# Making the last group's first dense product beside its keys and queries instead of inside the output phase

## The chip, the cores and the metric

The kernel runs on one core of one Trainium2 chip; the rounds of runs were on different chips, and in each the kernel before ran beside the others. The metric is the device time of one execution in microseconds (us). A ratio is the mean time of one kernel's fast runs over the mean of the other's fast runs of the same rounds, with a 95% interval; it is therefore not quite the ratio of the medians quoted beside it.

Engine names are those of the profile: PE (matrix products), PEld (loading a product's stationary operand), DVE (vector), ACT (activation functions), POOL, and SP, which starts most of the DMA transfers. A "product" below is one PE instruction, for example 128x128 times 128x512.

## The reference

The computation is `x + A(xn) + B(xn)` with `xn = layernorm(x)`, 2048 tokens of width 512 in bfloat16.

```python
xn = _layernorm(x)
# A: linear attention, 32 heads of width 16
q, k, v = split(xn @ wqkv)
phi_q = concat(softmax(q @ w_phi), softmax(-(q @ w_phi)))
phi_k = concat(softmax(k @ w_phi), softmax(-(k @ w_phi)))
kv, z = phi_k^T v, sum(phi_k)            # over all tokens
A = (phi_q kv) / (phi_q z + 1e-6) @ wo
# B: two dense products
h = xn @ w1 + b1                          # 512 -> 1792
B = (h * tanh(softplus(h))) @ w2          # Mish, 1792 -> 512
```

`kv` and `z` are sums over all tokens, so no attention output can be made before the keys of the last tokens are done. B has no such dependency.

## The kernel before: what matters here

The tokens are worked in 4 groups of 512. For each group the kernel makes keys and values (`stage_kv_pair`, twice), queries (`stage_q`), the layer norm of the next group (`stage_ln`), the group's share of the sums (`stage_kvacc`), and the first dense product with Mish (`stage_h`). Then comes the output phase: attention output (`stage_o`) and, accumulated in one PSUM tile, the second dense product and the product with `wo` (`stage_out`). Before the change, the last group's `stage_h` stands in the output phase.

```python
# PSUM, 128 x 512 fp32 is one bank
ps_kq = pool(bufs=2)   # tiles of 2 banks: pk, pq, ph, pnd   ("big")
ps_v  = pool(bufs=2)   # tiles of 1 bank:  pv, po, pf
ps_m  = pool(bufs=2)   # tiles of 1 bank:  pS, pkv, transposes

def stage_kv_pair(xnT, pr):          # 256 tokens
    pk = big("pk"); ...              # 8 products of 512 columns
    ek[:, 0] = Exp(pk); ek[:, 1] = Exp(-pk)                    # ACT
    for tt in range(2):
        pv = bank_v("pv"); ...       # 4 products
        ss = reduce_sum(ek); rk = reciprocal(ss)               # DVE
        v12[:, :, :, 0:DH] = pv * rk                           # DVE, frees pv
        ...
def stage_q(g, xnT):
    for jp in range(2):
        pq = big("pq"); ...          # 8 products
        eq[:, 0] = Exp(pq); eq[:, 1] = Exp(-pq)                # ACT
        ...                          # 4 times: pS = B16b x eq (PE), eqT = pS * eq (DVE)
def stage_h(xnT):
    act = apool.tile([P, FT, 512], BF16, name="act")
    for fp in range(FT // 2):        # 7 pairs
        ph = big("ph"); ...          # 8 products
        ...                          # 2 x act = Mish(ph + b1)   (ACT)
    return act
def stage_o(g):
    for t in range(TPG):
        pnd = big("pnd"); ...        # 8 products of 136 columns: eqT x kvm
        rd = reciprocal(...); o_t = pnd * rd                   # DVE
    ...                              # 16 transposes ptro (PE), 2 copies oT (ACT)
def stage_out(g, act, oT):
    for t in range(TPG):
        po = bank_v("po")
        ...                          # 14 products act x w2, then 4 products oT x wo
        y = po + x; store(y)

for g in range(NG):
    parts = [stage_kv_pair(xnT, pr) for pr in range(2)]
    ...
    stage_q(g, xnT)
    if g + 1 < NG:
        ...; xnTs[g + 1] = stage_ln(g + 1)
    stage_kvacc(g, parts)
    if g + 1 == NG:
        break
    acts[g] = stage_h(xnT)
... # kvm = masked sums (DVE)
for g in range(NG):
    oT = stage_o(g)
    stage_out(g, acts[g], oT)
    if g == 0:
        acts[NG - 1] = stage_h(xnTs[NG - 1])
```

The framework's scheduler decides at compile time in which order the stages' instructions stand on each engine. So the program's text is not the order on PE; below, orders are told as the compiled program has them. A product that waits holds up all products behind it: the Trainium skill, "PSUM — Partial Sum Buffer", section "Engine vs sequencer instructions", says that matrix products start and complete in program order, and the traces here agree: in the longest wait looked at in group 3 (2.91 us) no product starts on PE.

The softmax here doesn't subtract the row's maximum and nothing guards it: scores larger than these inputs give would overflow.

Of the kernel before, what the change touches and what calls it, by code (L numbers as in the profile page):

```python
# [8 lines left out]
BF16 = mybir.dt.bfloat16  # L9
# [8 lines left out]
def kernel(  # L18
# [13 lines left out]
    P = 128  # L32
    S, D, NH, DH, F = 2048, 512, 32, 16, 1792
    NG = 4
# [3 lines left out]
    FT = F // P  # L38
# [20 lines left out]
    xnpool = ctx.enter_context(tc.tile_pool(name="xn", bufs=4))  # L59
    xnTpool = ctx.enter_context(tc.tile_pool(name="xnT", bufs=2))  # L60
    spool = ctx.enter_context(tc.tile_pool(name="small", bufs=4))
    ekpool = ctx.enter_context(tc.tile_pool(name="ek", bufs=4))
    eqpool = ctx.enter_context(tc.tile_pool(name="eq", bufs=2))
    vpool = ctx.enter_context(tc.tile_pool(name="v12", bufs=6))
    apool = ctx.enter_context(tc.tile_pool(name="act", bufs=3))

    prep_w = tc.alloc_tile_pool(name="prep_w", bufs=1)
# [71 lines left out]
    def chain(ins):  # L139

        prev = last_of.get("act")
        last_of["act"] = ins
        if prev is not None:
            tc.add_manual_dep(
                ins.ins,
                prev.ins.name,
                mybir.DependencyInfo(
                    mybir.DependencyClass.NoSync, mybir.DependencyReason.DATA
                ),
                reason="table order",  # L150
            )

    def big(name):
        return ps_kq.tile([P, 2, 512], FP32, name=name, tag="kq")
# [8 lines left out]
    def stage_ln(g):  # L163
        xg = xgs[g]
        mv = spool.tile([P, TPG, nc.vector.BN_AGGR_DIM], FP32, name="mv")
        rstd = spool.tile([P, TPG], FP32, name="rstd")
        for t in range(TPG):
            st = spool.tile([P, nc.vector.BN_STATS_DIM], FP32, name="st")
            nc.vector.bn_stats(st[:], xg[:, t, :])  # L169
            nc.vector.bn_aggr(mv[:, t, :], st[:])  # L170
        chain(nc.scalar.activation(rstd[:], mv[:, :, 1], ACT.Sqrt, bias=eps_t[:]))  # L171
        nc.vector.reciprocal(rstd[:], rstd[:])
        xns = []
        for t in range(TPG):
            xn = xnpool.tile([P, D], BF16, name="xn")
            nc.vector.tensor_scalar(  # L176
                out=xn[:],
                in0=xg[:, t, :],
                scalar1=mv[:, t, 0:1],
                scalar2=rstd[:, t : t + 1],  # L180
                op0=ALU.subtract,
                op1=ALU.mult,
            )
            xns.append(xn)
        xnT = xnTpool.tile([P, KT, 512], BF16, name="xnT")
        for kh in range(2):
            ptr = bank_m("ptr", [P, 2, 512], BF16)
            for t in range(TPG):
                for k in range(2):
                    kt = 2 * kh + k  # L190
                    nc.tensor.transpose(  # L191
                        ptr[:, k, t * P : (t + 1) * P],
                        xns[t][:, kt * P : (kt + 1) * P],
                        ident[:],
                    )
            nc.scalar.copy(xnT[:, 2 * kh : 2 * kh + 2, :], ptr[:])
        return xnT
# [12 lines left out]
    def fold(src, dst):  # L210
        wTs = []
        for jh in range(2):
            ptr = bank_m("ptrw", [P, 2, 512], BF16)
            for jj in range(2):
                j = 2 * jh + jj
                for kt in range(KT):
                    nc.tensor.transpose(
                        ptr[:, jj, kt * P : (kt + 1) * P],
                        src[:, kt, j * P : (j + 1) * P],
                        ident[:],  # L220
                    )
            wT = prep_w.tile([P, 2, 512], BF16, name="wT", bufs=2)
            nc.scalar.copy(wT[:], ptr[:])
            wTs.append(wT)
        for kt in range(KT):
            pf = bank_v("pf")
            for j in range(4):
                nc.tensor.matmul(
                    pf[:, j * P : (j + 1) * P],
                    lhsT=wTs[j // 2][:, j % 2, kt * P : (kt + 1) * P],  # L230
                    rhs=Wbd[:, j, :],
                    start=True,
                    stop=True,
                )
            nc.vector.tensor_copy(dst[:, kt, :], pf[:])
# [76 lines left out]
    def stage_q(g, xnT):  # L312
        gs = slice(g * 512, (g + 1) * 512)
        for jp in range(2):
            pq = big("pq")
            for jj in range(2):
                j = 2 * jp + jj
                for kt in range(KT):
                    nc.tensor.matmul(  # L319
                        pq[:, jj, :],  # L320
                        lhsT=wqp[:, kt, j * P : (j + 1) * P],
                        rhs=xnT[:, kt, :],
                        start=(kt == 0),
                        stop=(kt == KT - 1),
                    )
            eq = eqpool.tile([P, 2, 2, 512], BF16, name="eq")
            chain(nc.scalar.activation(eq[:, 0], pq[:], ACT.Exp))  # L327
            chain(nc.scalar.activation(eq[:, 1], pq[:], ACT.Exp, scale=-1.0))  # L328
            for jj in range(2):
                j = 2 * jp + jj  # L330
                for pl in range(2):
                    pS = bank_m("pS")
                    nc.tensor.matmul(  # L333
                        pS[:],
                        lhsT=B16b[:],
                        rhs=eq[:, 1 - pl, jj, :],
                        start=True,
                        stop=True,
                    )
                    nc.vector.tensor_tensor(  # L340
                        out=eqT[:, pl * 4 + j, gs],
                        in0=pS[:],
                        in1=eq[:, pl, jj, :],
                        op=ALU.mult,
                    )


    def stage_h(xnT):
        act = apool.tile([P, FT, 512], BF16, name="act")
        for fp in range(FT // 2):  # L350
            ph = big("ph")
            for ff in range(2):
                f = 2 * fp + ff
                for kt in range(KT):
                    nc.tensor.matmul(  # L355
                        ph[:, ff, :],
                        lhsT=w1_sb[:, kt, f * P : (f + 1) * P],
                        rhs=xnT[:, kt, :],
                        start=(kt == 0),
                        stop=(kt == KT - 1),  # L360
                    )
            for ff in range(2):
                f = 2 * fp + ff
                chain(
                    nc.scalar.activation(  # L365
                        act[:, f, :], ph[:, ff, :], ACT.Mish, bias=b1f[:, f : f + 1]
                    )
                )
        return act
# [68 lines left out]
    xnTs = [None] * NG  # L438
    acts = [None] * NG
# [5 lines left out]
    for g in range(NG):  # L445
        xnT = xnTs[g]
        parts = [stage_kv_pair(xnT, pr) for pr in range(2)]
        if g == 0:
            fold(wq_raw, wqp)
            prep_w.release()  # L450
            oTpool = ctx.enter_context(tc.tile_pool(name="oT", bufs=2))
            rpool = ctx.enter_context(tc.tile_pool(name="rden", bufs=4))
            opool = ctx.enter_context(tc.tile_pool(name="o_t", bufs=5))
            ypool = ctx.enter_context(tc.tile_pool(name="y", bufs=3))
        stage_q(g, xnT)
        if g + 1 < NG:
            if g + 1 > 1:
                xgs[g + 1] = xpool.tile([P, TPG, D], BF16, name="xg")
                nc.sync.dma_start(xgs[g + 1][:], x_g[g + 1])
            xnTs[g + 1] = stage_ln(g + 1)  # L460
        stage_kvacc(g, parts)
        if g + 1 == NG:
            break
        acts[g] = stage_h(xnT)

    kvv = kvacc[:].rearrange("p s (h v) -> p s h v", v=VW)
    nc.vector.tensor_scalar(
# [12 lines left out]
    for g in range(NG):  # L480
        oT = stage_o(g)
        stage_out(g, acts[g], oT)
        if g == 0:
            acts[NG - 1] = stage_h(xnTs[NG - 1])


# [28 lines left out]
```

## Time and profile before

| | before |
|---|---|
| median time, 3 runs | 231.58 us |
| span of the profiled run | 229.3 us |
| PE busy | 197.9 us, 86% |

These lines are of the profile's page: PE's busy time and instructions, PE's busy tenths in 40 slices of the span, the granted PE clock in tenths, and the engines' shares of the chain that ended last.

```profile
PE 197.9 (86%) x1185; PEld 99.1 (43%) x1185; DVE 120.2 (52%) x205; ACT 101.3 (44%) x124; POOL 8.5 (4%) x26
...
PE   0089168889999999999999599899999999999993
...
PEclk9999977999999999999999979999999999999999
...
PE 61%; ACT 18%; DVE 12%; issue 4%; DMA 3%; SPq 1%; ACTq 0%
```

Counting the slices from 0, PE is busy 90% or more in every slice from 9 on except 22, 25 and the last, and it carries 61% of the chain. There is one dent left, in slices 22 to 25 (126 to 149 us), with a clock of 7 tenths in one slice: the last group's keys and queries and the start of the output phase.

The timeline there (start, duration, engine, line, instruction, count; in brackets the engine's idle time before it and what ended it):

```profile
127.17 1.89 PE L258 MATMUL pv<-wv,xnT 128*128 128x512 bf16 x8
...
130.76 1.17 DVE L274 TENSOR_TENSOR v_1202<-pv,rk 128x1024 bf16<-128x1024 f32 x1
...
131.97 3.54 PE L418 MATMUL po<-w_sb,act 128*128 128x512 bf16 x9 [2.91 <-DVE v_1202 L274]
...
143.24 1.11 PE L380 MATMUL pnd<-kvm,eqT 128*128 128x136 bf16 x16 [0.23 <-DVE kvm L474]
...
145.05 0.65 PE L380 MATMUL pnd<-kvm,eqT 128*128 128x136 bf16 x8 [0.71 <-DVE o_t L391]
...
146.53 0.90 PE L403 MATMUL ptro<-ident,o_t 128*128 128x128 bf16 x8
...
147.27 1.03 PE L355 MATMUL ph<-xnT,w_sb 128*128 128x512 bf16 x4
```

Two gaps are to be seen. First: the second `pv` ends at about 129.1 us, and the next work on PE is the first output product `po`. It needs a PSUM bank of `ps_v`, and both are held by `pv` until DVE has made `v_1202`. PE stands for 2.91 us. After it, 9 products take 3.54 us. Second: from 143.2 to 147 us `pnd` waits for `kvm` (0.23 us) and for `o_t` (0.71 us), and the transposes `ptro` come one by one with DVE's `o_t`; only 4 dense products (`ph`) stand between the last of them, and 5 more behind.

The windows table (stretch; length; busy time and count of each engine; granted PE clock; DMA share and GB/s), with stretches cut at these places:

```profile
core 0: us, PE busy (x) PEld busy (x) DVE busy (x) ACT busy (x) POOL busy (x), PEclk, DMA share, GB/s
...
129.06:131.97 2.91, 0.00 (x1) 0.00 (x0) 2.91 (x5) 0.00 (x0) 0.86 (x2) 0.92 0.00 0
131.97:135.14 3.17, 3.17 (x9) 1.09 (x9) 2.27 (x3) 0.00 (x0) 0.00 (x0) 0.54 0.00 0
...
149.51:170.15 20.64, 20.64 (x96) 9.21 (x96) 2.67 (x4) 9.74 (x14) 0.00 (x0) 1.00 0.15 51
170.15:188.13 17.98, 17.96 (x117) 9.04 (x116) 6.08 (x11) 3.19 (x4) 0.00 (x0) 1.00 0.07 23
```

The rows are the wait (PE busy 0.00 us of 2.91), the 9 products after it (granted clock 0.54), the first output group from its first `wo` product to the end of the late dense product, and the second output group from its first to the third's first `pnd`. In the last two PE is busy all the time. At full rate one product of 512 columns starts every 0.216 us (40 take 8.63 us), at half rate every 0.43 us.

### The profile page before, as it was taken

What the parts mean: (1) busy time and instruction counts of PE and PEld (TensorE: products, weight loads), DVE (VectorE), ACT (ScalarE), POOL (GpSimd) and SP (SyncE); (2) the same over time, 40 slices, a digit from 0 to 9 for tenths busy, and PEclk for the clock granted to TensorE, in tenths of its full rate; (3) what the DMA queues carried; (4) which work ended last, traced back from release to release, by engine and by line L of the source; (5) the groups of instructions that cost most, each with busy time, mean ns of one, the idle gap of its engine ahead of it and who ended that gap; (6) DMA issues with size and microseconds to landing.
All of it is one profiled execution on the core that took longest, in us unless ns stands there. A gap on an engine that the chain in (4) does not pass through costs nothing.

```text
span 229.3 us, 2898 instructions
## 1 busy us (share of the span) xinstructions
PE 197.9 (86%) x1185; PEld 99.1 (43%) x1185; DVE 120.2 (52%) x205; ACT 101.3 (44%) x124; POOL 8.5 (4%) x26
## 2 busy tenths in 40 slices
PE   0089168889999999999999599899999999999993
PEld 0065024355444364443644236544455455446441
DVE  1538798667069951699516978622015226217121
ACT  0266500995889677896778400142663002000300
POOL 2000110000011000110001100000000000000000
PEclk9999977999999999999999979999999999999999
DMA  6999100011000030000200000010300103010001
GB/s 169 363 363 348 43 0 0 1 46 48 0 0 1 0 93 2 0 0 3 91 0 3 0 0 1 0 49 23 114 0 3 46 23 117 23 46 26 23 26 43
DMA packets 12120, 12.25 MB, mean 53 GB/s; under 512 B 1100, under 2 KB 12108, under 8 KB 12108
## 3 DMA queue, kind: packets, MB, share of 16 engines
q1 hardware_dynamic: 10496, 11.01, 14.6%
q10 hardware_dynamic: 1612, 1.07, 1.7%
q8 instruction: 9, 0.15, 0.3%
q14 instruction: 3, 0.02, 0.0%
HBM read 9.98 MB, written 2.10 MB: 53 GB/s over the span
## 4 chain that ended last, share of the span: by engine, by line
PE 61%; ACT 18%; DVE 12%; issue 4%; DMA 3%; SPq 1%; ACTq 0%
PE po L418 21%; PE ph L355 17%; PE po L426 6%; DVE ss L266 5%; PE pkv L294 3%; ACT act L365 3%; PE pq L319 3%; PE pnd L380 3%; DMA xg<-in_A_x_dram 3%; ACT L251 2%; ACT L171 2%; PE ptr L191 2%; ACT ek L252 2%; ACT ek L251 2%; ACT eq L327 2%
## 5 line engine op out<-in xcount | busy, mean ns | idle before, releaser
L418 PE MATMUL po<-w_sb,act 128*128 128x512 bf16 x224 | 56.0, 386 | 2.9 <-DVE v_1202 L274 2.9
L355 PE MATMUL ph<-xnT,w_sb 128*128 128x512 bf16 x224 | 54.7, 379 | 1.7 <-ACT act L365 1.7
L365 ACT ACTIVATE act<-ph,b1f 128x512 bf16<-128x512 f32 x56 | 35.2, 686 | 22.9 <-PE ph L355 15.7
L434 DVE TENSOR_TENSOR y<-po,xg 128x512 bf16<-128x512 f32 x16 | 11.0, 691 | 44.7 <-PE po L426 44.7
L418 PEld LDWEIGHTS <-act 128*128 128x128 bf16 x224 | 21.7, 99 | 27.3 <-issue 5.5
L355 PEld LDWEIGHTS <-w_sb 128*128 128x128 bf16 x224 | 21.6, 98 | 26.4 <-issue 2.7
L408 ACT COPY oT<-ptro 128x1024 bf16<-128x1024 bf16 x8 | 7.7, 1015 | 56.3 <-PE ptro L403 56.3
L266 DVE TENSOR_REDUCE ss<-ek 128x64 f32<-128x1024 bf16 x16 | 18.7, 1212 | 24.2 <-ACT ek L252 24.2
L340 DVE TENSOR_TENSOR eqT<-pS,eq 128x512 bf16<-128x512 f32 x32 | 20.5, 687 | 4.1 <-PE pS L333 4.1
L258 PE MATMUL pv<-wv,xnT 128*128 128x512 bf16 x64 | 16.9, 404 | 4.8 <-DVE v_260 L274 4.8
L319 PE MATMUL pq<-xnT,wqp 128*128 128x512 bf16 x64 | 16.6, 405 | 0.9 <-ACT ek L252 0.9
L426 PE MATMUL po<-wo_sb,oT 128*128 128x512 bf16 x64 | 16.9, 380 | 0.0
L191 PE MATMUL ptr<-ident,xn 128*128 128x128 bf16 x64 | 6.1, 242 | 11.3 <-DVE xn L176 11.3
L243 PE MATMUL pk<-wkp,xnT 128*128 128x512 bf16 x64 | 15.4, 379 | 0.0
L327 ACT ACTIVATE eq<-pq 128x1024 bf16<-128x1024 f32 x8 | 8.2, 1027 | 14.9 <-PE pq L319 14.3
L169 DVE BATCH_NORM_STATS2 st<-xg 128x6 f32<-128x512 bf16 x16 | 10.5, 674 | 5.9 <-DMA xg<-in_A_x_dram 5.9
L333 PE MATMUL pS<-eq,B16b 128*128 128x512 bf16 x32 | 11.5, 378 | 0.9 <-ACT eq L328 0.9
L258 PEld LDWEIGHTS <-xnT 128*128 128x128 bf16 x64 | 6.5, 102 | 13.2 <-issue 6.2
L389 DVE RECIPROCAL rd<-pnd 128x32 f32<-128x32 f32 x16 | 5.6, 349 | 11.5 <-PE pnd L380 11.5
L391 DVE TENSOR_TENSOR o_t<-pnd,rd 128x512 bf16<-128x512 f32 x16 | 11.1, 692 | 0.5
L319 PEld LDWEIGHTS <-wqp 128*128 128x128 bf16 x64 | 6.6, 104 | 9.2 <-issue 3.1
L380 PE MATMUL pnd<-kvm,eqT 128*128 128x136 bf16 x128 | 9.6, 223 | 1.1 <-DVE o_t L391 0.7
(96 smaller groups left out, 197.0 us busy)
## 6 DMA issues: line engine op xcount, KB each, us to landing
xg<-in_A_x_dram SPq DMA_DIRECT2D x7, 512.0 KB, 4.0
out_dram<-y SPq DMA_DIRECT2D x16, 128.0 KB, 1.7
w_sb<-in_B_w_dram SPq DMA_DIRECT2D x2, 896.0 KB, 7.8
w_sb<-in_B_w_dram SPq DMA_DIRECT2D x1, 1792.0 KB, 13.5
wk_raw<-in_A_wqkv_dram ACTq DMA_DIRECT2D x1, 512.0 KB, 4.6
xg<-in_A_x_dram SPq DMA_DIRECT2D x4, 128.0 KB, 4.8
wq_raw<-in_A_wqkv_dram ACTq DMA_DIRECT2D x1, 512.0 KB, 6.9
wv<-in_A_wqkv_dram SPq DMA_DIRECT2D x1, 512.0 KB, 7.2
```

What stands on the lines that cost most here:

```text
L243: nc.tensor.matmul(pk[:, tt, :], lhsT=xnT[:, kt, tok0 : tok0 + P], rhs=wkp[:, kt, :], start=(kt == 0), stop=(kt == KT - 1),)
L258: nc.tensor.matmul(pv[:], lhsT=xnT[:, kt, tok0 : tok0 + P], rhs=wv[:, kt, :], start=(kt == 0), stop=(kt == KT - 1),)
L266: nc.vector.reduce_sum(ss[:], ek[:, :, tt, :].rearrange("p s (h e) -> p s h e", e=DH), axis=AX.X,)
L319: nc.tensor.matmul(pq[:, jj, :], lhsT=wqp[:, kt, j * P : (j + 1) * P], rhs=xnT[:, kt, :], start=(kt == 0), stop=(kt == KT - 1),)
L327: chain(nc.scalar.activation(eq[:, 0], pq[:], ACT.Exp))
L333: nc.tensor.matmul(pS[:], lhsT=B16b[:], rhs=eq[:, 1 - pl, jj, :], start=True, stop=True,)
L340: nc.vector.tensor_tensor(out=eqT[:, pl * 4 + j, gs], in0=pS[:], in1=eq[:, pl, jj, :], op=ALU.mult,)
L355: nc.tensor.matmul(ph[:, ff, :], lhsT=w1_sb[:, kt, f * P : (f + 1) * P], rhs=xnT[:, kt, :], start=(kt == 0), stop=(kt == KT - 1),)
L365: nc.scalar.activation(act[:, f, :], ph[:, ff, :], ACT.Mish, bias=b1f[:, f : f + 1])
L380: nc.tensor.matmul(pnd[:, j // 2, (j % 2) * 136 : (j % 2) * 136 + 136], lhsT=eqT[:, pl * 4 + j, tok0 : tok0 + P], rhs=kvm[:, pl * 4 + j, : ...
L418: nc.tensor.matmul(po[:], lhsT=act[:, f, ts], rhs=w2_sb[:, f, :], start=(f == 0), stop=False,)
L426: nc.tensor.matmul(po[:], lhsT=oT[:, j, ts], rhs=wo_sb[:, j, :], start=False, stop=(j == 3),)
```

## The change

The intent: make the last group's first dense product next to its keys and queries, as in the other groups, so that PE has independent work there. All four activation tiles then live at once, so a fourth buffer is needed, and other pools are cut to make room in SBUF.

```diff
-    ekpool = ctx.enter_context(tc.tile_pool(name="ek", bufs=4))
+    ekpool = ctx.enter_context(tc.tile_pool(name="ek", bufs=3))
-    vpool = ctx.enter_context(tc.tile_pool(name="v12", bufs=6))
+    vpool = ctx.enter_context(tc.tile_pool(name="v12", bufs=5))
...
-    def stage_h(xnT):
-        act = apool.tile([P, FT, 512], BF16, name="act")
+    def stage_h(xnT, pool):
+        act = pool.tile([P, FT, 512], BF16, name="act")
...
             prep_w.release()
+            apool3 = ctx.enter_context(tc.tile_pool(name="act3", bufs=1))
...
-            opool = ctx.enter_context(tc.tile_pool(name="o_t", bufs=5))
-            ypool = ctx.enter_context(tc.tile_pool(name="y", bufs=3))
+            opool = ctx.enter_context(tc.tile_pool(name="o_t", bufs=4))
+            ypool = ctx.enter_context(tc.tile_pool(name="y", bufs=2))
...
         stage_kvacc(g, parts)
-        if g + 1 == NG:
-            break
-        acts[g] = stage_h(xnT)
+        acts[g] = stage_h(xnT, apool if g + 1 < NG else apool3)
...
         stage_out(g, acts[g], oT)
-        if g == 0:
-            acts[NG - 1] = stage_h(xnTs[NG - 1])
```

## The prediction

It was made before the changed kernel had run, from the profile of before and the compiled orders of both.

> **What bounds the kernel now.** The tensor engine. The page gives PE 86% of the span, and the chain of waits is 61% PE. From 149.5 us to the last product (windows 149.51 to 225.81) PE is busy without a gap; DVE and ACT are mostly idle there. In that stretch a 512-column product starts every 0.216 us (40 of the dense product take 8.63 us in the chain). So only idle or slow PE time can be saved; the change removes no PE work (both orders hold 1185 products).
>
> **Where PE time is lost before.** Group 3 and the start of the output phase, 117.54 to 149.51, hold 93 products of 512 columns, 64 of 136 and 16 transposes: my estimate at the full rate is 93x0.216 + 64x0.060 + 16x0.056 = 24.8 us, against 31.97 us. Of the 7.2 us lost:
> - 2.9 us: PE stands from 129.1 to 131.97, because the first output product needs a PSUM bank that DVE frees at the end of v_1202 (table of waits, timeline);
> - about 1.8 us: after this gap the granted clock is 0.50 from 132 to 134.9 us (windows) and products start every 0.43 us. The Trainium skill, "TensorE: Matmul & The Clock Gate", section "What's actually happening", says an idle PE falls to half clock; the trace agrees, after about 2.5 us idle;
> - about 1.8 us: from 142.9 to 148.1 kvm and then pnd to o_t to transposes run with little other PE work queued;
> - 0.5 us: second pq waits for ACT's exponentials; the rest is small change.
>
> **What the change moves.** By the compiled order, group 3's 56 dense products now fill the place after the second pv, as in group 2: pv x4, ph x2, pv x4, ph x14, po x4, ph x5, then ph between the pS; 24 more stand between pkv and the first pnd. All four output groups then have the order that group 1's has now. The smaller pools (ek 3, v12 5, o_t 4, y 2) add waits that should already be met: each buffer's last reader is done microseconds earlier. The fourth activation buffer only permits the move. Table loads stay equal in number.
>
> **Sum.** Everything up to the second pv of group 3 stays (pS starts at 126.75). Then pS, pv, ph 26 products to 132.35; po x4 needs its bank, free at 131.93, so no stall and no clock drop; ph x5, then 17 products to 138.0; pkv about 2.3 us to 140.3; ph x24 5.2 us to 145.5 (kvacc and kvm, 1.75+0.2+1.3 us on DVE, hide under it). From the first pnd on, the order equals before's from 170.15 us, plus one more output group of 18.74 us (188.13 to 206.87). Span: 145.5 + (229.3-170.15) + 18.74 = 223.3 us against 229.3, 6.0 us less. ACT is no limit: group 2 with its square root keeps a 28.7 us period, and group 3 has none (1.6 us less).
>
> Predicted time 225.6 us, range 224.7 to 227.1. Chances: faster by over 2% 0.86, within 2% 0.13, slower by over 2% 0.01. The order barely leaves room for a loss; the doubt is whether 2% (226.95 us) is passed.
>
> **What would show it.** No 2.9 us PE wait on v_1202's counterpart, granted clock 1.00 around 132 us, first pnd at about 145.5 us with no wait on kvm, four output groups of 18.0 to 18.9 us each, PE busy total slightly lower, last product ending near 220 us.
>
> **What would make it wrong.** The po x4 standing on DVE after all (its margin is about 0.4 us), with another clock drop; ph waiting on mish in group 3 as it does 0.55 us in group 2; a wait from the smaller pools (a y buffer on its store, or a v12 in groups 1 to 3) that appears in earlier groups; stage_o(0) no longer hidden.

## The result, and the profile after

The changed kernel took 226.07 us (median of 4 runs, 225.44 to 226.62); the kernel before 231.63 us beside it. The ratio is 0.9749 (0.9713 to 0.9786): 2.5% faster. Repeated with more rounds on another occasion it was 226.83 us, ratio 0.9743 (0.971 to 0.9777).

The same lines of the page after:

```profile
PE 197.7 (88%) x1185; PEld 100.1 (45%) x1185; DVE 120.4 (54%) x205; ACT 101.2 (45%) x124; POOL 8.6 (4%) x26
...
PE   0089455889999999999999999999999999999993
...
PEclk9999967999999999999999999999999999999999
...
PE 70%; ACT 15%; DVE 8%; DMA 2%; issue 2%; SPq 1%; ACTq 0%
```

PE's busy time is the same, as no work was removed. The dent in the slices of the last group is gone and PE's share of the chain rose from 61% to 70%: from 126.1 us to the last product the chain now runs on PE, where before it ran on ACT and DVE until 131.97 us and again from 140.7 to 147.0 us, but for 0.65 us of `pnd`. The clock's dip in the middle is gone; one near the start (slices 5 and 6), which before has too, remains.

The timeline of the same place:

```profile
130.51 3.19 PE L355 MATMUL ph<-xnT,w_sb 128*128 128x512 bf16 x14
...
131.87 1.17 DVE L274 TENSOR_TENSOR v_1205<-pv,rk 128x1024 bf16<-128x1024 f32 x1
...
133.53 1.03 PE L418 MATMUL po<-w_sb,act 128*128 128x512 bf16 x4
...
141.31 5.34 PE L355 MATMUL ph<-xnT,w_sb 128*128 128x512 bf16 x24
...
146.49 0.64 PE L380 MATMUL pnd<-kvm,eqT 128*128 128x136 bf16 x8
...
146.96 1.03 PE L418 MATMUL po<-w_sb,act 128*128 128x512 bf16 x4
...
148.00 1.11 PE L380 MATMUL pnd<-kvm,eqT 128*128 128x136 bf16 x16
```

Where PE stood idle there are now sixteen dense products, 2 between the halves of the second `pv` and 14 right behind it. `v_1205`, the counterpart of `v_1202`, ends at 133.04 us (131.87 + 1.17), and the first `po` starts at 133.53 us without a wait. Behind the sums (`pkv`) come 24 dense products while DVE makes `kvm`, and between the `pnd` there are now `po` products.

The windows: from the end of the second `pv` to the third `pS`, from there to the first `pnd`, and the first output group:

```profile
130.50:135.47 4.97, 4.97 (x24) 2.25 (x23) 4.86 (x7) 3.33 (x5) 0.88 (x2) 1.00 0.00 0
135.47:146.49 11.02, 11.02 (x75) 5.93 (x74) 6.83 (x11) 5.06 (x8) 0.00 (x0) 1.00 0.00 1
146.49:164.47 17.98, 17.96 (x118) 9.06 (x116) 6.08 (x11) 3.19 (x4) 0.00 (x0) 1.00 0.07 23
```

PE is busy throughout and the clock is 1.00. The last row is the first output group, from its first `pnd` to the next group's first `pnd`: 17.98 us, exactly what the second output group took before.

The profiled spans differ by 5.0 us, but the profiled run of after happened to reach group 3 later: its first `pk` of group 3 comes at 118.67 us, before's at 117.54 us. In all profiled runs of kernels that do not change group 0 or the start, this point lies anywhere between 117.1 and 119.5 us, with either set of buffers. So I compare from the first `pk` of group 3 to the end of the span (the span minus that start): **111.76 us before, 105.63 us after, 105.67 us in the repeated run**. The difference, 6.1 us, is what the change did; the repeated run shows that this measure holds within 0.04 us, while whole times spread by some 1%. The spans are given to 0.1 us, so a difference of less than about 0.1 us in it says nothing.

### The profile page after: what moved, and what is told of

Same layout as the page of the kernel before. It is cut to its first block, busy times and chain, and to the rows that moved or that the text cites. A ratio compares the mean times of both kernels' runs of the same rounds, so it can differ in the third digit from the quotient of the medians.

```text
span 224.3 us, 2903 instructions
## 1 busy us (share of the span) xinstructions
PE 197.7 (88%) x1185; PEld 100.1 (45%) x1185; DVE 120.4 (54%) x205; ACT 101.2 (45%) x124; POOL 8.6 (4%) x26
## 3 DMA queue, kind: packets, MB, share of 16 engines
q1 hardware_dynamic: 10496, 11.01, 15.0%
## 4 chain that ended last, share of the span: by engine, by line
PE 70%; ACT 15%; DVE 8%; DMA 2%; issue 2%; SPq 1%; ACTq 0%
PE po L418 22%; PE ph L355 17%; PE po L426 6%; DVE ss L266 5%; PE pkv L294 4%; PE pnd L380 4%; PE pq L319 3%; PE pv L258 3%; PE pk L243 3%; ACT eq L328 2%; DMA xg<-in_A_x_dram 2%; ACT L171 2%; PE pS L333 2%; PE ptr L191 2%; ACT ek L252 2%
## 5 line engine op out<-in xcount | busy, mean ns | idle before, releaser
L355 PE MATMUL ph<-xnT,w_sb 128*128 128x512 bf16 x224 | 55.5, 379 | 1.7 <-ACT act L365 1.7
L418 PE MATMUL po<-w_sb,act 128*128 128x512 bf16 x224 | 54.4, 379 | 0.0
L418 PEld LDWEIGHTS <-act 128*128 128x128 bf16 x224 | 21.2, 98 | 22.2
L243 PE MATMUL pk<-wkp,xnT 128*128 128x512 bf16 x64 | 15.9, 387 | 0.0
L327 ACT ACTIVATE eq<-pq 128x1024 bf16<-128x1024 f32 x8 | 8.2, 1028 | 14.9 <-PE pq L319 14.3
L191 PEld LDWEIGHTS <-xn 128*128 128x128 bf16 x64 | 4.4, 106 | 12.6 <-DVE xn L176 11.9
L196 ACT COPY xnT<-ptr 128x1024 bf16<-128x1024 bf16 x8 | 7.7, 1015 | 5.0 <-PE ptr L191 5.0
```

What stands on the lines that cost most here:

```text
L191: nc.tensor.transpose(ptr[:, k, t * P : (t + 1) * P], xns[t][:, kt * P : (kt + 1) * P], ident[:],)
L243: nc.tensor.matmul(pk[:, tt, :], lhsT=xnT[:, kt, tok0 : tok0 + P], rhs=wkp[:, kt, :], start=(kt == 0), stop=(kt == KT - 1),)
L355: nc.tensor.matmul(ph[:, ff, :], lhsT=w1_sb[:, kt, f * P : (f + 1) * P], rhs=xnT[:, kt, :], start=(kt == 0), stop=(kt == KT - 1),)
L418: nc.tensor.matmul(po[:], lhsT=act[:, f, ts], rhs=w2_sb[:, f, :], start=(f == 0), stop=False,)
```

## The experiments

The theory before the experiments: two stretches are filled, the wait for `v12` with the half clock behind it (4.6 us by the prediction's sum), and the stretch of `kvm`, `pnd` and `o_t` (about 1.8 us). Rivals: the gain comes from getting the dense product out of the output phase; or from the changed buffers; or the first gap is all.

| run | what | median us | ratio to before (95%) | first pk of group 3 to end of span, us |
|---|---|---|---|---|
| before | | 231.58 | 1 | 229.3 - 117.54 = 111.76 |
| after_again | the change | 226.83 | 0.9743 (0.971-0.9777) | 225.1 - 119.43 = 105.67 |
| e1_pools | buffers alone | 231.26 | 0.9982 (0.9918-1.0047) | 230.2 - 118.58 = 111.62 |
| e2_early4 | 4 of 7 pairs moved | 226.99 | 0.9748 (0.9713-0.9784) | 224.7 - 118.81 = 105.89 |
| e3_afterkv | moved, but behind the sums | 231.53 | 0.9962 (0.9913-1.001) | 229.0 - 117.53 = 111.47 |
| e4_junk | before, idle time filled with useless products | 231.26 | 0.9926 (0.9887-0.9964) | 229.8 - 119.52 = 110.28 |
| e5_bare | the change, output products used up early | 227.56 | 0.9805 (0.9748-0.9862) | 224.3 - 117.08 = 107.22 |

The medians are of different rounds; the median of before beside them was 232.95 us for after_again, e2_early4, e3_afterkv and e4_junk, and 232.25 us for e1_pools and e5_bare. The last column rests on one profiled run of each.

### The change again (after_again)

> The changed kernel once more, with more rounds. My theory (two stretches of idle or slow TensorE around the last group's keys and queries are filled, 5.9 us in all): ratio to before 0.972 to 0.977, and the group 3 stretch repeats (no PE wait for v12, clock 1.00, first pnd about 27.8 us after the first pk of group 3). Second question: the profiled run of the changed kernel spent 1.1 us more before group 1 (half-rate products from 12 to 19 us) than that of before. If that is chance of the clock at the start, this profile shows some other start, between 60.1 and 61.2 us for the first pk of group 1; if it belongs to the changed pools, it is at 61.2 us again.

Measured: 0.9743, clock 1.00, first `pnd` 27.81 us (147.24 - 119.43) after the first `pk`. On the second question, the first `pk` of group 1 came at 61.95 us, later than either; in e3_afterkv, with the same buffers, it came at 60.05 us. So the 1.1 us at the start belong to the single execution and not to the change.

### Buffers alone (e1_pools)

```diff
 # against the changed kernel
-        acts[g] = stage_h(xnT, apool if g + 1 < NG else apool3)
+        if g + 1 == NG:
+            break
+        acts[g] = stage_h(xnT, apool)
...
         stage_out(g, acts[g], oT)
+        if g == 0:
+            acts[NG - 1] = stage_h(xnTs[NG - 1], apool3)
```

> Only the buffers of the change (ek 3, v12 5, o_t 4, y 2, a fourth activation buffer), while the last group's dense product stays in the output phase. My theory: the buffers alone do nothing; ratio to before 0.995 to 1.005, first pnd 25.7 us after the first pk of group 3, and 111.8 us from that pk to the end of the span. Rival, that the smaller pools gain or lose time: outside that.

Measured: 0.9982, first `pnd` 25.56 us after the first `pk` (144.14 - 118.58), 111.62 us to the end. The buffers alone do nothing that can be seen (0.14 us).

### Four of the seven pairs (e2_early4)

```diff
 # against the changed kernel; stage_h takes a range of pairs
-        acts[g] = stage_h(xnT, apool if g + 1 < NG else apool3)
+        if g + 1 < NG:
+            acts[g] = stage_h(xnT, apool)
+        else:
+            acts[g] = stage_h(xnT, apool3, range(4))
...
         stage_out(g, acts[g], oT)
+        if g == 0:
+            stage_h(xnTs[NG - 1], apool3, range(4, FT // 2), acts[NG - 1])
```

> Half of the move: 4 of the 7 pairs of the last group's first dense product go next to keys and queries, 3 pairs stay in the output phase, pools as after. The compiled order then has dense products after the second pv as in the changed kernel, but after pkv come 9 output products instead of 24 dense ones. My theory: the first gap (2.9 us idle, 1.8 us of half clock) is gone, and the second (kvm, pnd, o_t) is filled too, by the output products which are no longer used up in the first: ratio 0.974 to 0.978, within 0.7 us of the changed kernel. Rival, that the second gap needs the dense product itself, or that the output phase runs better only without any dense product in it: only the first gap's 4.6 us are won, ratio 0.980 or higher.

Measured: 0.9748, 105.89 us, 0.24 us from the changed kernel. PE's timeline in this run:

```profile
141.45 2.10 PE L419 MATMUL po<-w_sb,act 128*128 128x512 bf16 x9
143.58 1.12 PE L381 MATMUL pnd<-kvm,eqT 128*128 128x136 bf16 x16
144.53 1.03 PE L419 MATMUL po<-w_sb,act 128*128 128x512 bf16 x4
145.40 0.65 PE L381 MATMUL pnd<-kvm,eqT 128*128 128x136 bf16 x8
```

Behind the sums now stand output products, no dense ones, and they cover `kvm` as well; `po` fills between the `pnd`. So three of the seven pairs can stay in the output phase at hardly any cost, and the rival that the output phase must be rid of dense products falls.

### The whole product, but behind the sums (e3_afterkv)

```diff
 # against the changed kernel: each first ph of the last group gets an
 # order-only dependency on the last pkv product
-            acts[g] = stage_h(xnT, apool if g + 1 < NG else apool3)
+            acts[g] = stage_h(xnT, apool3, last_of["pkv"])   # for g + 1 == NG
```

> The other half: the whole dense product is made before the output phase, but ordered behind the last pkv product, so that it cannot fill the gap after the second pv. Pools as after. My theory: the 2.9 us wait for v12 and the half clock after it are still there, and only the second gap (about 1.8 us, less 0.3 us that every output group loses) is won: ratio 0.992 to 0.996, about 230.1 us. Rival, that the gain comes from the dense product having left the output phase, wherever it goes: ratio near 0.975.

Measured: 0.9962 (0.9913 to 1.001), 111.47 us: 0.29 us won, not the 1.5 us I expected. The rival is refuted far more clearly, but my own number was wrong too. PE's timeline:

```profile
131.96 3.49 PE L428 MATMUL po<-w_sb,act 128*128 128x512 bf16 x9 [2.86 <-DVE v L274]
...
145.58 8.80 PE L355 MATMUL ph<-xnT,w_sb 128*128 128x512 bf16 x40
154.21 0.64 PE L390 MATMUL pnd<-kvm,eqT 128*128 128x136 bf16 x8
...
157.54 0.65 PE L390 MATMUL pnd<-kvm,eqT 128*128 128x136 bf16 x8 [0.48 <-DVE o_t L401]
```

The first wait is there as before (2.86 us), as it should be. `kvm` is hidden behind dense products: DVE ends it at 143.1 us, 11 us before the first `pnd`. But the `pnd` and transposes run just as bare as before: a wait of 0.48 us on `o_t`. The compiled order tells why: of the 28 `po` products that can be made without attention output (two tiles of 14, because `ps_v` has two banks) 25 had been used up before the first `pnd`, from 131.96 us on, and the last 3 right behind it. Dense products can't step in, because none are left: all 56 stand ahead of the first `pnd` here. (In the kernel before they come later, and yet only 4 stand among the transposes; by the code `ph` needs the `ps_kq` tiles that `pnd` holds, which would explain it, but no run tests this.) So I mended the theory: what the second gap lacks is not dense products behind the sums but output products kept back for `stage_o`. In the changed kernel the dense products do the filling beside the queries, and that saves the output products for later. The Trainium skill, "PSUM — Partial Sum Buffer", section "Specifications (TRN2)", gives 8 banks per partition; the three pools take 4 + 2 + 2 of them, so there was no bank to give either stage.

### The mended theory's test (e5_bare)

```diff
 # against the changed kernel
+    # the 28 w2 products of po tiles 0 and 1 of group 0 are issued first ...
+        if g == 0:
+            for t in range(2):
+                po, behind = po_dense(acts[0], t)
+                ready.append(po)
+        # ... and the first pnd gets an order-only dependency on the last of them
-        oT = stage_o(g)
-        stage_out(g, acts[g], oT)
+        oT = stage_o(g, behind)
+        stage_out(g, acts[g], oT, ready)
```

> The changed kernel with the move kept, but 28 output products (all that two PSUM banks hold without attention output) ordered ahead of the first pnd, so that the first stage_o has no output product left to run beside it. The first gap stays filled. Theory as mended after the run behind pkv, which gained 0.3 us and not 1.5: the second loss is not that dense products are missing after pkv, but that output products, the only work that fits beside pnd (dense products need the PSUM buffers that pnd holds), have been used up by then. Then this kernel gives back 1.0 to 1.6 us: from the first pk of group 3 to the end of the span 106.7 to 107.3 us against 105.65, ratio to before 0.979 to 0.983. Rival, that filling the first gap is all: 105.4 to 105.9 us, ratio near 0.974.

Measured: 107.22 us, 1.57 us given back, ratio 0.9805. PE's timeline shows the bare chain again, 4 output products having been made beside the queries and the other 24 here ahead of the first `pnd`:

```profile
144.90 5.34 PE L425 MATMUL po<-w_sb,act 128*128 128x512 bf16 x24
150.08 1.11 PE L380 MATMUL pnd<-kvm,eqT 128*128 128x136 bf16 x16
151.90 0.65 PE L380 MATMUL pnd<-kvm,eqT 128*128 128x136 bf16 x8 [0.71 <-DVE o_t L402]
```

The 0.71 us wait on `o_t` is back, to the hundredth the one of before. The first gap stays filled in this kernel, so filling it is not all; the second gap is worth about 1.6 us. This rests on the trace: the whole times (226.06 to 228.76 us) overlap those of after_again, and by them alone the run is unclear. The scheduler also brought some `pnd` of the next group forward into the bare stretch, so the 1.57 us is the net loss.

### Useless products in the wait (e4_junk)

```diff
 # against the kernel before
         stage_q(g, xnT)
+        if g + 1 == NG:
+            pj = big("junk")
+            for i in range(12):
+                nc.tensor.matmul(pj[:, i // 6, :], lhsT=w1_sb[:, i % 4, 0:P],
+                                 rhs=xnT[:, i % 4, :], start=(i % 6 == 0), stop=(i % 6 == 5))
```

> The kernel before, with 12 useless products of 512 columns (2.6 us of work, into a PSUM buffer that nobody reads; the result stays right) put where PE waits for v12 in group 3. My theory: they fit into the 2.9 us wait, so they cost nothing, and they keep the clock at 1.00 afterwards, which saves the about 1.8 us of half-rate output products: ratio 0.991 to 0.994, about 229.8 us. Rival, that the half clock is not caused by this gap or costs nothing: same as before or slower, ratio 0.999 to 1.012, with the granted clock still 0.5 for some 3 us after.

Measured: 0.9926, 110.28 us, 1.48 us less than before, with 12 products more. PE's timeline:

```profile
131.31 2.32 PE L459 MATMUL junk<-xnT,w_sb 128*128 128x512 bf16 x10
133.95 2.10 PE L418 MATMUL po<-w_sb,act 128*128 128x512 bf16 x9 [0.32 <-DVE v L274]
```

And the windows of one microsecond in which those 9 products run:

```profile
134.00:135.00 1.00, 1.00 (x5) 0.44 (x5) 1.00 (x2) 0.00 (x0) 0.00 (x0) 1.00 0.00 0
```

The wait shrank to 0.32 us, because useless work took its place, and the 9 output products behind it take 2.10 us instead of 3.54 us. The granted clock is 1.00 in every microsecond from 128 to 136 us. So the half clock does come from the gap and costs 1.5 us by itself; I had put it at 1.8 us.

### The lesson carried to group 0 (h4, h4_again, h5)

Group 0 has bigger gaps of the same kind. This is PE's timeline of the kernel before:

```profile
28.71 3.22 PE L258 MATMUL pv<-wv,xnT 128*128 128x512 bf16 x8 [4.79 <-DVE v_260 L274]
34.05 0.38 PE L228 MATMUL pf<-Wbd,wT 128*128 128x128 bf16 x4 [2.11 <-DVE v_296 L274]
...
37.31 4.20 PE L319 MATMUL pq<-xnT,wqp 128*128 128x512 bf16 x14
```

The waits of 4.79 and 2.11 us are the long ones; 8 `pv` then take 3.22 us and 14 `pq` 4.20 us, where 0.216 us each would be 1.7 and 3.0 us. ACT is idle for 14.3 us there (it waits for `pq`, by the table of waits). The Trainium skill, "Perfetto Trace Analysis", section "Optimization Strategy", advises interleaving where the busiest engine changes between stages; these traces agree, in that DVE sets the pace in this stretch (11.63 us busy of the 12 from 24 to 36 us) and PE (4.22 us) does not. The edit makes 4 of the 7 pairs of group 0's dense product before its queries:

```diff
 # against the changed kernel; stage_h takes a range of pairs, as above
         if g == 0:
+            acts[0] = stage_h(xnT, apool, range(4))
             fold(wq_raw, wqp)
...
-        acts[g] = stage_h(xnT, apool if g + 1 < NG else apool3)
+        acts[g] = stage_h(xnT, apool if g + 1 < NG else apool3,
+                          range(4 if g == 0 else 0, FT // 2), acts[g])
```

> The lesson carried to group 0: 4 of the 7 pairs of its dense product are made between its keys and its queries, where PE now stands some 9 us between 24 and 42 us and then runs at half clock for about 6 us. Theory: 6.9 us of dense products leave the stretch after the queries and go into that idle time, and the clock stays up, for one more table load on ACT (1.28 us, in a stretch where ACT is idle 14 us): 6 to 9 us less than the changed kernel, ratio to before 0.938 to 0.952. Rival: DVE, busy without a break there, sets the pace and the transposes for group 1 come too late: under 4 us, ratio over 0.957.

Measured: 218.26 us (217.54 to 218.30), ratio 0.94 (0.9358 to 0.9442), by the ratios some 8 us less than the changed kernel (0.974). PE's timeline:

```profile
26.16 3.72 PE L356 MATMUL ph<-xnT,w_sb 128*128 128x512 bf16 x16 [0.36 <-ACT ek L252]
...
32.64 3.19 PE L356 MATMUL ph<-xnT,w_sb 128*128 128x512 bf16 x14
...
38.42 3.28 PE L319 MATMUL pq<-xnT,wqp 128*128 128x512 bf16 x14
```

The 32 dense products took the idle time, and 14 `pq` now take 3.28 us. The kernel's second half is as after: 216.6 - 110.92 = 105.68 us from the first `pk` of group 3.

> The version with 4 of 7 pairs of group 0's dense product between its keys and queries, once more, beside its two variants on the same chip: ratio to before 0.937 to 0.943, spread of its runs under 1 us (the kernel before spreads by 3 us), because the stretches of half clock in group 0 are gone.

Measured: 217.79 us (217.26 to 218.31), ratio 0.937 (0.9339 to 0.9401); the runs spread over 1.05 us, the kernel before beside it over 2.6 us. The forecast for these was under 1 us and about 3 us. The mean granted clock of each run: 0.998 to 1.000 in these six; in the eleven of before beside them, the five with 0.978 took 230.73 to 232.31 us and the six with 0.963 or 0.970 took 232.65 to 233.34 us. So the spread goes with the stretches of half clock, as the reason has it, though a mean clock does not say where in the kernel they lie. In the rounds of h4 this is less clean (two runs of before with 0.970 took 231.0 and 231.4 us).

> 5 pairs instead of 4. There is about 1.1 us of idle PE left between the dense products and the folds of wq, and 4 fewer than 8 products stand behind pkv, so a fifth pair (1.7 us of work) half fits: 0 to 1.2 us less than with 4 pairs. Rival: with nothing left to make beside the transposes for group 1, PE waits for their copies (1.93 us on ACT) and the gain is lost: 0 to 1 us more.

(That text has a slip: with 4 pairs one dense product stands behind the sums, and with 5 none.) Measured: 219.61 us, ratio 0.9431 (0.9389 to 0.9474), 1.8 us slower than 4 pairs on the same chip by the medians. The rival's direction was right. Its size (0 to 1 us) was right for three of the six runs, those with a mean clock of 1.000 (218.09 to 219.11 us, median 0.6 us slower); the other three had 0.992 and took 220.10 to 220.22 us. The profiled run is one of these. PE's timeline, and the windows of the same place:

```profile
49.37 1.36 PE L191 MATMUL ptr<-ident,xn 128*128 128x128 bf16 x16 [0.67 <-DVE xn L176]
51.73 1.42 PE L294 MATMUL pkv<-v,ek 128*128 128x136 bf16 x12 [0.99 <-ACT xnT L196]
53.38 2.27 PE L294 MATMUL pkv<-v,ek 128*128 128x136 bf16 x20 [0.22 <-issue]
```

```profile
51.70:53.40 1.70, 1.45 (x13) 1.39 (x15) 0.21 (x1) 1.68 (x2) 0.00 (x0) 0.56 0.84 283
```

PE waits for `xn` (0.67 us) and for its copies (0.99 us), as the rival has it; and then the clock falls to half while `pkv` runs, which nobody had expected and which, by the mean clocks, half of the runs have. Too much had been moved out of this place.

### The clock at the start (w_after, w_h4)

```diff
 # against the changed kernel, and against h4
+    warm = prep_w.tile([P, 512], BF16, name="warm")
+    nc.vector.memset(warm[:], 1.0)
+    pw = bank_m("pw")
+    for i in range(28):
+        nc.tensor.matmul(pw[:], lhsT=warm[:, 0:P], rhs=warm[:], start=(i == 0), stop=(i == 27))
```

> The changed kernel with 28 useless products of 512 columns at the start, while PE has nothing to do before the first transposes at about 11 us. In the traces so far the first pk of group 3 comes anywhere between 117.5 and 119.5 us, in kernels with either set of pools, and the late ones have half-rate products from 12 to 20 us. Theory: that scatter is the TensorE clock still at half rate at the start; then the useless products bring it up before 11 us, the first pk of group 3 comes at 117.5 us or earlier, and the median is 0.5 to 1.5 us below the changed kernel's: ratio to before 0.968 to 0.973. Rival, that loads arriving late make the scatter: no change, ratio 0.974 to 0.977.

Measured: 225.66 us (224.32 to 227.53), ratio 0.974 (0.9682 to 0.9798): inconclusive. The first `pk` of group 3 came at 117.33 us in the profiled run, as the theory has it, but the runs spread by 3.2 us all the same.

> 4 pairs, and the 28 useless products at the start. Left open by the run of the changed kernel with them, whose interval was too wide: if half-rate products from 12 to 20 us cost time, this one is 0.8 to 1.6 us faster than 4 pairs alone on the same chip (the profiled run with 4 pairs had its first pk at 20.0 us, the one with useless products at 18.3 us). Rival: within 0.4 us, because something else sets the pace there.

Measured: 216.19 us (216.00 to 217.53), ratio 0.9319 (0.9284 to 0.9355), 1.6 us below h4_again by the medians, though the two sets of runs overlap slightly. With the useless products, 4 products of 128 columns take 0.40 us, and the first `pk` of the kernel comes at 18.27 us:

```profile
15.73 0.40 PE L240 MATMUL pf<-Wbd,wT 128*128 128x128 bf16 x4 [0.23 <-ACT wT L235]
```

Without them (h4), the same 4 take 0.61 us, and the first `pk` comes at 20.00 us:

```profile
16.07 0.61 PE L228 MATMUL pf<-Wbd,wT 128*128 128x128 bf16 x4 [0.19 <-ACT wT L223]
```

Of these 1.73 us, 0.34 us had been lost before the first transposes, which start at 11.35 us in h4 and at 11.01 us in w_h4. In h4_again they start at 10.97 us, and the first `pk` comes at 19.62 us, 1.35 us later than in w_h4; so late loads do not explain that part. The half rate at the start costs about 1.6 us by the medians where group 0 doesn't add its own scatter. This is the fastest kernel, 6.8% below the kernel before in the same rounds; its result is right.

## Why the prediction was right

- **Direction, size and chances.** 225.6 us were predicted with a range of 224.7 to 227.1; 226.07 us were measured. That the two lie within 0.5 us is partly luck, since whole times spread by some 2 us and the repeated run's median was 226.83 us; the saving is the sounder test. The predicted saving of 6.0 us in the span compares with 6.1 us from the first `pk` of group 3 on. The order of instructions was known from the compiled program, and each stretch had a measured counterpart elsewhere in the trace of before (group 2 for group 3, the second output group for the first): that is why so small a change could be told to a few tenths.
- **First gap.** "2.9 us: PE stands from 129.1 to 131.97": gone after. The predicted margin of about 0.4 us between the bank's release and the `po` was 0.49 us (133.53 - 133.04).
- **Half clock.** "About 1.8 us" was 1.5 us (e4_junk): right in kind, a little large.
- **Second gap.** "About 1.8 us: from 142.9 to 148.1" is 0.3 us for `kvm` (e3_afterkv) and 1.6 us for the bare `pnd` chain (e5_bare), 1.9 us together. The prediction's sum was right because it took over the second output group's 17.98 us. But it did not name what does the filling. It reads as if 24 dense products behind the sums did it; e3_afterkv showed that those hide `kvm` alone, and e2_early4 that they are not needed. The dense products work indirectly, by keeping output products back.
- **The whole.** 1.48 us for the clock, 0.29 us for `kvm` and 1.57 us for the chain, taken from 6.13 us (111.76 - 105.63), leave, if the shares simply add, 2.8 us for the idle wait itself, which the table of waits puts at 2.9 us. That last share was not isolated by a run of its own; it is what remains.
- **Doubts that did not come true.** No wait from the smaller buffers (e1_pools), and none of `ph` on Mish in group 3.
- **First pnd.** Predicted at about 145.5 us, measured at 146.49 us, because that run's group 3 began 1.13 us later; from the first `pk` on, 27.96 us were predicted (145.5 - 117.54) and 27.82 us measured.
- **Left open.** Why whole times of before and after spread by 1%: part is the clock at the start (w_h4), part lies in group 0. There the traces have half clock for 6.8 us in before and after, about 10.2 us in after_again, e4_junk and e5_bare, and none in h4. How much of the spread each makes was not measured.

## What to carry to other kernels

When an engine that is the bottleneck stands still, ask which independent work could be queued in front of the waiting instruction, and which buffers that work needs: work that needs the very buffers under contention cannot fill the gap (here the first `po` waited 2.91 us for its bank). Filler is limited, so spend first the kind that fits only there, and keep the kind that will be needed in the next gap. Count a gap at more than its length where the clock falls behind it (here 2.9 us of waiting plus 1.5 us), and look for the same pattern elsewhere in the kernel: in group 0 it was worth more than the change itself (ratio 0.937 to 0.940 with it, 0.974 without).

## What the Trainium skill lacked or had wrong

- "TensorE: Matmul & The Clock Gate", section "What's actually happening", gives half clock after at least one idle window of about 3.4 us. Here the clock fell sooner: at 131.5 us after 2.4 us without a product (before), at 11.9 us in w_h4 after 1.5 us without one and 0.9 us with some, and at 51.9 us in h5, where the gaps had been 0.67 and 0.99 us. So the window need not be idle throughout: the 3.41 us before these falls held 0.97, 1.80 and 1.74 us of products. The length of a half-clock stretch does agree with the page's window: 131.5 to 134.9 us, 29.1 to 32.5 us (before) and 51.9 to 55.3 us (h5), about 3.4 us each. The changes of before (29.1, 32.5, 35.9, 39.3, 131.5 and 134.9 us) all lie on one grid of 3.41 us, whatever the gaps' own starts; so in these traces it also mattered where on the grid a gap fell.
- The same page, section "Seeing it yourself", warns that the clock's trace events can be unreliable; it doesn't say how this shows at the start. In h4 the granted clock is recorded as 1.00 from 12 to 20 us, in the line below, while four products of 128 columns take 0.61 us instead of 0.40 us. Here the products' spacing is the better witness.

```profile
12.00:20.00 8.00, 6.97 (x58) 6.01 (x59) 2.97 (x8) 3.85 (x4) 0.00 (x0) 1.00 1.08 356
```

- The same page, section "What's actually happening", puts the cost of the warm-up at the start under 1% of a typical span. This agrees: it was about 1.6 us of 217.8 us (0.7%). But the remark is on the start alone; here one gap's clock cost another 1.48 us of 231.6 us (0.6%).
- No page says that of two kinds of filler the one that fits the next gap should be kept back; here that was worth 1.57 us (e5_bare).
